# Attention and experts on one core: weights of the next units converted early and parked in DRAM, one stream of work units, sink fill moved ahead of the branch

## The chip, the cores and the metric

One core of one Trainium2 chip runs the whole program. The metric is the device time of one execution in microseconds (us). Its engines work side by side and meet through semaphores: TensorE (PE, matmuls), VectorE (DVE), ScalarE (ACT), GpSimd (POOL) and SyncE (SP), whose queue issues all DMAs here. Each engine works through its own queue in a fixed order.

## The reference

Three layers follow each other, all in float32 at the interface:

```python
# attention: 2 batches, 8 heads, 768 positions, head size 64; 4 sinks, window 128
scores = scale * np.matmul(q, k.transpose(0, 1, 3, 2))
keep = is_sink | in_window
a = softmax(np.where(keep, scores, -1e9))
x = (a @ v), reshaped to 1536 tokens x 512

# first layer: w_in 512 x 2048, w_out 2048 x 512, both given in float64
h = x @ w_in
g = h * np.tanh(softplus(h))          # mish
x = g @ w_out

# second layer: 4 experts, w1 512 x 1024, w2 1024 x 512, weighted by p
out += p[:, e:e+1] * (np.maximum(x @ w1[e], 0) @ w2[e])
```

## The kernel before

**Words.** Every matmul of the two last layers is done as three matmuls of parts: a number is split into a high part, which TensorE's fast float32 format holds, and a low part (`hi`, `lo`; names ending in h and l). So each weight matrix lies in SBUF twice. The first layer's weights come as float64. `split_double` (line 99) turns 1 MB of them into two parts of 512 KB by bit operations: one Abs on ACT (line 112), seven steps on DVE (lines 113 to 115 and 117 to 120), and a transfer of the high part (line 116) from the buffer `cv_h` to its place. This is called a conversion here. The buffers `cv_a`, `cv_r` and `cv_h` exist once.

**Attention.** It runs over 24 items: 2 batches, 3 blocks of 256 rows (i = 0, 1, 2), 4 pairs of heads. An item (`attention_item`, line 209) has four score matmuls (`sc`), a masked minimum on DVE (line 228), Exp on ACT, a reciprocal on DVE, the multiplication by it on POOL (lines 246 and 249), transposes (`tp`), and the products with v and with the sinks' v (`pv`). It ends with `xl` on DVE (line 179), by which items can be told in the trace. Its loads of q, k and v are asked for two items ahead. The sinks' v is filled and loaded by `sink_values` (line 132), within the branch that the flag in line 653 selects.

**Work units.** The first layer is cut into units 0 to 3 of 512 hidden columns, the second into units 4 to 11. One unit needs a first matrix `wi` (`wih`, `wil`) and a second, `wo`. `stream` (line 434) interleaves layer 1 of one chunk of tokens with layer 2 of the chunk before: chunks of 256, 256, 512 and 512 tokens for unit 0, three of 512 for all others. Layer 1 (line 450) makes four blocks `h` of 128 hidden columns, 12 matmuls each, in PSUM; `mish` (line 528) turns each into `gh` and `gl`: five activations on ACT with three DVE steps between them (540, 542, 543; the last one, `w`, is the last reader of `h`), then gh on ACT and gl on POOL. Layer 2 makes blocks `o` of 12 matmuls from the four gh and gl. Unit 0 runs within the attention from item 5 on, with one PSUM bank for h and one for o; after it there are three each. A pool of four pairs of g tiles serves the attention; three more are added behind it (`more_g`).

**Weights before.** While the attention runs, unit 0's four conversions and the two of unit 1's wi are asked for (m < 4, 8, 11). The two of unit 1's wo, and all eight of units 2 and 3, come behind it, the latter while the unit before runs (`rest`, line 591). The conversions write straight into SBUF; units 0 and 2 share one set of places, 1 and 3 the other.

**Order.** A scheduler with a model of the engines' times sets the order of each queue when the program is built. The source above gives it the dependencies and the priorities.

## Time and profile before

| | us |
|---|---|
| median of 3 runs (lowest, highest) | 960.02 (959.64, 961.45) |
| profiled execution | 957.99 |
| its span | 956.1 |
| PE busy | 922.4 (96%) |
| DVE busy | 421.3 (44%) |
| ACT busy | 350.1 (37%) |
| POOL busy | 273.4 (29%) |

The span is cut into 40 slices of 23.9 us on the profile's page. From 350 us to the last slice TensorE's digit is 9 in all of them; the lower ones all lie before. The attention's last DVE step starts at 173 us, the first matmul of the second layer's products (L515) at 445 us. In a stretch, PEclk is the granted TensorE clock as a share of full speed: 1.00 is 2.4 GHz, 0.50 is 1.2 GHz, and a value between is a mixture of both. A busy PE counts from an instruction's start to its modelled end, so a busy share near 100% can hide slower work.

### The profile page before, as it was taken

Reading aid. Unit: us, or ns where it says so; the run is one execution under the profiler, and the core shown is the slowest. Engines: PE = TensorE matmul, PEld = TensorE weight load, DVE = VectorE, ACT = ScalarE, POOL = GpSimd, SP = SyncE. Lnnn points to the kernel's source line nnn. Section 1 sums busy time; section 2 is a strip of 40 time slices with the busy share of each in tenths; the row PEclk is TensorE's granted clock in tenths of the full one; section 3 lists DMA queues with packets and bytes.
Section 4 is the critical chain, followed back from the end, with each engine's and each line's share of the span. In section 5 each row is a group of like instructions: output and inputs, shape, how many; then the busy total and the mean of one; then the engine's idle time right before and its main releaser. Section 6 shows DMA issues by size and latency. Waiting matters only on the chain.

```text
span 956.1 us, 11114 instructions
## 1 busy us (share of the span) xinstructions
PE 922.4 (96%) x4292; PEld 737.6 (77%) x4292; DVE 421.3 (44%) x754; ACT 350.1 (37%) x745; POOL 273.4 (29%) x233
## 2 busy tenths in 40 slices
PE   8998999878899999999999999999999999999997
PEld 5566577657688788888888888888888888888886
DVE  6898732189859745673112222222222222222222
ACT  4686774477576667852221111111111111111110
POOL 5786831122132245343022211220220222200000
PEclk7798999989899999999999999999999999999999
DMA  7654500033403101011011011110110110000012
GB/s 233 228 190 159 195 18 1 1 113 129 155 23 133 66 23 45 23 45 45 0 45 45 8 38 45 44 41 4 45 45 1 44 45 1 1 1 1 11 45 81
DMA packets 31198, 57.59 MB, mean 60 GB/s; under 512 B 3856, under 2 KB 12304, under 8 KB 31136
## 3 DMA queue, kind: packets, MB, share of 16 engines
q1 hardware_dynamic: 31136, 56.79, 17.9%
q8 instruction: 36, 0.59, 0.3%
q14 instruction: 26, 0.21, 0.1%
HBM read 45.25 MB, written 3.15 MB: 51 GB/s over the span
## 4 chain that ended last, share of the span: by engine, by line
PE 83%; DVE 11%; issue 2%; DMA 1%; ACT 1%; POOL 1%; SPq 0%; DVEq 0%; POOLq 0%; ACTq 0%
PE h L462 38%; PE o L515 27%; PE o L491 9%; PE sc L225 3%; PE pv L271 3%; PE tp L258 2%; DVE cv_h L115 2%; DVE cv_a L119 1%; DVE u L542 1%; DVE cv_a L117 1%; DVE w L543 1%; PE pv L277 1%; DVE u L540 1%; DVE cv_r L118 1%; DVE wol L120 1%
## 5 line engine op out<-in xcount | busy, mean ns | idle before, releaser
L462 PE MATMUL h<-xh,wih 128*128 128x512 f32 (+1 forms) x592 | 231.0, 390 | 13.0 <-DVE w L543 12.6
L462 PE MATMUL h<-xh,wil 128*128 128x512 f32 (+1 forms) x592 | 228.9, 387 | 0.0
L462 PE MATMUL h<-xl,wih 128*128 128x512 f32 (+1 forms) x592 | 228.1, 387 | 0.0
L473 ACT ACTIVATE gh<-h 128x512 fp32r<-128x512 f32 x96 | 57.3, 598 | 408.3 <-PE h L462 243.5
L474 DVE SCALAR_TENSOR_TENSOR gl<-h,gh 128x512 fp32r<-128x512 f32 x96 | 66.3, 692 | 207.8 <-ACT gh L473 207.8
L515 PE MATMUL o<-wol,gh 128*128 128x512 f32 (+1 forms) x388 | 150.1, 387 | 0.0
L515 PE MATMUL o<-woh,gh 128*128 128x512 f32 (+1 forms) x388 | 150.1, 387 | 0.0
L515 PE MATMUL o<-woh,gl 128*128 128x512 f32 (+1 forms) x388 | 149.9, 387 | 0.0
L462 PEld LDWEIGHTS h<-xh,wih 128*128 128x128 f32 x592 | 112.6, 190 | 39.7 <-DVE w L543 15.4
L523 DVE SCALAR_TENSOR_TENSOR acc<-o,pn,acc 128x512 f32<-128x512 f32 (+1 forms) x85 | 63.3, 745 | 176.2 <-PE o L515 176.2
L462 PEld LDWEIGHTS h<-xl,wih 128*128 128x128 f32 x592 | 112.3, 190 | 23.3 <-issue 1.1
L462 PEld LDWEIGHTS h<-xh,wil 128*128 128x128 f32 x592 | 112.6, 190 | 21.7
L96 POOL TENSOR_TENSOR gl<-w,gh 128x512 fp32r<-128x512 f32 (+1 forms) x52 | 69.7, 1344 | 186.8 <-ACT gh L88 182.9
L491 PE MATMUL o<-gh,woh 128*128 128x512 f32 (+1 forms) x208 | 79.6, 383 | 5.5 <-ACT gh L88 5.4
L515 PEld LDWEIGHTS o<-wol,gh 128*128 128x128 f32 x388 | 72.9, 188 | 14.9
L515 PEld LDWEIGHTS o<-woh,gh 128*128 128x128 f32 x388 | 72.9, 188 | 14.9
L515 PEld LDWEIGHTS o<-woh,gl 128*128 128x128 f32 x388 | 72.8, 188 | 14.7
L491 PE MATMUL o<-gh,wol 128*128 128x512 f32 (+1 forms) x208 | 78.5, 378 | 0.0
L491 PE MATMUL o<-gl,woh 128*128 128x512 f32 (+1 forms) x208 | 73.9, 380 | 0.0
L86 POOL TENSOR_SCALAR wih<-stage 128x1024 fp32r<-128x1024 f32 x16 | 16.5, 1052 | 193.7 <-PE h L462 193.7
L540 DVE SCALAR_TENSOR_TENSOR u<-w,r 128x512 f32<-128x512 f32 (+1 forms) x52 | 33.4, 643 | 64.4 <-ACT r L539 64.3
L86 POOL TENSOR_SCALAR woh<-stage 128x1024 fp32r<-128x1024 f32 x16 | 16.5, 1053 | 137.1 <-PE o L515 122.1
(82 smaller groups left out, 1125.3 us busy)
## 6 DMA issues: line engine op xcount, KB each, us to landing
stage<-in_moe_w_dram SPq DMA_DIRECT2D x32, 512.0 KB, 3.7
stage<-in_moe_w_in_dram SPq DMA_DIRECT2D x8, 1024.0 KB, 5.8
stage<-in_moe_w_out_dram SPq DMA_DIRECT2D x8, 1024.0 KB, 5.0
qk<-in_qk_dram SPq DMA_DIRECT2D x16, 324.0 KB, 3.3
wih<-cv_h SPq DMA_DIRECT2D x8, 512.0 KB, 3.2
woh<-cv_h SPq DMA_DIRECT2D x8, 512.0 KB, 2.9
acc<-in_v_dram SPq DMA_DIRECT2D x16, 192.0 KB, 2.6
out_dram<-acc SPq DMA_DIRECT2D x11, 256.0 KB, 2.1
```

The source lines that it names most:

```text
L86: eng.tensor_scalar(out, src, 1.0, 0.0, ALU.mult, ALU.add)
L96: eng_lo.tensor_tensor(lo, src, hi.bitcast(F32), ALU.subtract)
L115: nc.vector.scalar_tensor_tensor(h, w_hi, -0x40000000, a, ALU.bitwise_and, ALU.bitwise_or)
L225: nc.tensor.matmul(sc, lhsT=raw[rows, t * P:(t + 1) * P], rhs=raw[rows, k0:k0 + sw], start=True, stop=True)
L271: nc.tensor.matmul(pv[64 * j:64 * j + 64, q0:q0 + ns * P], lhsT=v[:, blk, j * c.D:(j + 1) * c.D], rhs=pts[j][:, sg:sg + ns], start=n == 0, ...
L462: nc.tensor.matmul(h, lhsT=wis[sw][:, k, fs], rhs=x[sx][:, k, cols], start=k == 0 and t == 0, stop=k == KT - 1 and t == 2,)
L473: nc.scalar.activation(gh, h, AF.Relu)
L474: nc.vector.scalar_tensor_tensor(gl, h, 0.0, gh.bitcast(F32), ALU.max, ALU.subtract)
L491: nc.tensor.matmul(o, lhsT=wos[sw][:, f, ds], rhs=g[f][sx], start=f == 0 and t == 0, stop=f == NF - 1 and t == 2,)
L515: nc.tensor.matmul(o, lhsT=g[f][sx][:, ds], rhs=wos[sw][:, f, ms], start=f == 0 and t == 0, stop=f == NF - 1 and t == 2,)
L523: nc.vector.scalar_tensor_tensor(y, o, pcol, y, ALU.mult, ALU.add)
L540: nc.vector.scalar_tensor_tensor(u, w, 1.0, r, ALU.add, ALU.mult)
```

## The change

- **Parking.** A new `park` converts unit 1's wi and wo and unit 2's wi, six conversions, while the attention runs (items 8, 10, 12, 14, 16 and 18), and writes both halves to DRAM. `split_double` gets a buffer `cv_l` for the low half and one more transfer (line 126 of the kernel after). `weights` loads the halves back (line 434), two transfers of 512 KB per conversion. Unit 2's wo and unit 3's weights are converted as before.
- **Space.** Unit 1's wi no longer lies in SBUF during the attention; both its matrices are placed behind it. All seven pairs of g tiles exist from the start.
- **One stream.** Unit 0's chunks and all later units form one stream.
- **Sinks.** `sink_values` is called ahead of the branch.
- **Softmax multiplies.** For items with i = 0 the two multiplies of the first head of the pair go to DVE, those of the second stay on POOL.

```diff
@@ split_double
+    park = lo
+    if lo.dtype != F32R:
+        lo = pool.tile([P, n], F32R, tag="cv_l", name="cv_l")
...
-    nc.sync.dma_start(out=hi.bitcast(F32), in_=h.bitcast(F32))
+    nc.sync.dma_start(out=hi if lo is not park else hi.bitcast(F32), in_=h.bitcast(F32))
...
     nc.vector.scalar_tensor_tensor(lo, af, 2.0 ** -23, rf, ALU.mult, ALU.mult)
+    if lo is not park:
+        nc.sync.dma_start(out=park, in_=lo.bitcast(F32))
@@ attention_pools
-    a.vsk = sink_values(c, a)
+    a.vsk = c.vsk
@@ attention_item
-                nc.gpsimd.tensor_scalar(o, o, sm[:, 2 * j + t:2 * j + t + 1], None, ALU.mult)
+                (nc.gpsimd if j else nc.vector).tensor_scalar(o, o, sm[:, 2 * j + t:2 * j + t + 1], None, ALU.mult)
@@ Experts
-        self.gp = []
-        self.more_g(ctx, 4)
+        self.gp = ctx.enter_context(tp(name="m_g", bufs=7))
...
+    def park(self, pool, n, nm):
+
+        w = self.units[n][2 + (nm == "wo")]
+        hi, lo = self.parked[n, nm] = [pool.tile([P, self.KT, self.FU], F32, name=f"{nm}{n}{x}") for x in "hl"]
+        for k in range(0, self.KT, 2):
+            split_double(self.c, self.cv, hi[:, k:k + 2], lo[:, k:k + 2], load_double(self.c, w, k))
+            yield
...
+            if (n, nm) in self.parked:
+                for k in range(0, KT, 2):
+                    for t, d in zip((hi, lo), self.parked[n, nm]):
+                        nc.sync.dma_start(out=t[:, k:k + 2].bitcast(F32), in_=d[:, k:k + 2])
+                    yield
+            elif kind == 0:
@@ banded
-    x.wpool[1]["wi"] = ctx.enter_context(tc.tile_pool(name="m_1wi", bufs=1))
-    w = chain(x.weights(0), x.weights(1))
+    w = x.weights(0)
...
-    steps = x.stream([(0, 0, QW), (0, QW, QW)] + [(0, t0, x.CW) for t0 in range(2 * QW, c.T, x.CW)])
+    steps = x.stream([(0, 0, QW), (0, QW, QW)] + [(0, t0, x.CW) for t0 in range(2 * QW, c.T, x.CW)] + later(c, x, 1))
+    dram = ctx.enter_context(tc.tile_pool(name="park", bufs=1, space=bass.MemoryType.DRAM))
+    w = chain(w, x.park(dram, 1, "wi"), x.park(dram, 1, "wo"), x.park(dram, 2, "wi"))
...
-        if m < 4 or m in (8, 11):
+        if m < 4 or m in PARK:
...
-    x.wpool[1]["wo"] = ctx.enter_context(tc.tile_pool(name="m_1wo", bufs=1))
-    x.more_g(ctx, 3)
+    x.wpool[1] = ctx.enter_context(tc.tile_pool(name="m_w1", bufs=1))
     x.psum(ctx, 3, 3, 2)
-    run(w)
-    run(steps)
-    rest(c, x)
+    run(x.weights(1))
+    run(steps, 4 * (x.NF + 4) - 4 - (len(items) - LAG))
+    rest(c, x, steps, 1)
@@ swa_mish_experts_kernel, ahead of the branch
     mask_parts(c)
+    c.vsk = sink_values(c)
```

What this does to the order is seen best on DVE. First, the scores of item 18 in DVE's queue, before (L228 is the masked minimum of one score tile, `pr`; L542 and L543 are mish of a block of unit 0; the small second row of each minimum is left out):

```order
L228 ISA pr_1519,mx_1520<-sc_1522,mask260_90 128x260
L228 ISA pr_1519,mx_1520<-sc_1526,mask260_90 128x260
L542 SCALAR_TENSOR_TENSOR u_827<-u_827,r_828 128x256
L543 SCALAR_TENSOR_TENSOR w_826<-u_827,h_811 128x256
L228 ISA pr_1519,mx_1520<-sc_1530,mask260_90 128x260
L228 ISA pr_1519,mx_1520<-sc_1534,mask260_90 128x260
L179 TENSOR_TENSOR xl_92<-pv_1266,xh_91 128x256
```

And the scores of item 18 now (L234 is the same minimum, L117 to L123 are steps of a conversion):

```order
L117 TENSOR_SCALAR cv_a_1292<-cv_a_1292 128x1024
L234 ISA pr_1568,mx_1569<-sc_1571,mask260_90 128x260
L118 TENSOR_SCALAR cv_a_1292<-cv_a_1292 128x1024
L234 ISA pr_1568,mx_1569<-sc_1575,mask260_90 128x260
L119 SCALAR_TENSOR_TENSOR cv_h_1294<-stage_60,cv_a_1292 128x1024
L240 RECIPROCAL sm_1486<-sm_1486 128x4
L121 TENSOR_SCALAR cv_a_1292<-cv_h_1294 128x1024
L122 TENSOR_SCALAR cv_r_1293<-cv_h_1294 128x1024
L123 SCALAR_TENSOR_TENSOR cv_a_1292<-stage_60,cv_a_1292 128x1024
```

Between the scores of one item there stand five or more steps of a conversion now, where none stood.

Second, DVE's queue behind the attention, from mish of the first block of unit 0's last chunk on, before (wol is unit 1's second matrix, low half):

```order
L120 SCALAR_TENSOR_TENSOR wol_1997<-cv_a_1999,cv_r_2000 128x1024
L540 SCALAR_TENSOR_TENSOR u_2054<-w_2053,r_2055 128x512
L113 TENSOR_SCALAR cv_a_2012<-cv_a_2012 128x1024
L542 SCALAR_TENSOR_TENSOR u_2054<-u_2054,r_2055 128x512
L114 TENSOR_SCALAR cv_a_2012<-cv_a_2012 128x1024
L543 SCALAR_TENSOR_TENSOR w_2053<-u_2054,h_2038 128x512
L115 SCALAR_TENSOR_TENSOR cv_h_2014<-stage_60,cv_a_2012 128x1024
L117 TENSOR_SCALAR cv_a_2012<-cv_h_2014 128x1024
L118 TENSOR_SCALAR cv_r_2013<-cv_h_2014 128x1024
L540 SCALAR_TENSOR_TENSOR u_2082<-w_2081,r_2083 128x512
L119 SCALAR_TENSOR_TENSOR cv_a_2012<-stage_60,cv_a_2012 128x1024
```

The same place now (L553, L555 and L556 are the three steps of mish):

```order
L553 SCALAR_TENSOR_TENSOR u_2099<-w_2098,r_2100 128x512
L555 SCALAR_TENSOR_TENSOR u_2099<-u_2099,r_2100 128x512
L556 SCALAR_TENSOR_TENSOR w_2098<-u_2099,h_2083 128x512
L553 SCALAR_TENSOR_TENSOR u_2127<-w_2126,r_2128 128x512
L555 SCALAR_TENSOR_TENSOR u_2127<-u_2127,r_2128 128x512
L556 SCALAR_TENSOR_TENSOR w_2126<-u_2127,h_2111 128x512
```

The conversion steps between the steps of mish are gone from this place; the next one (L124) stands behind mish of the third block of unit 1.

Third, SP's queue at the end of the attention, before (the last loads of q, k and v, then the high halves of unit 1's wo):

```order
L128 DMA qk_1754<-in_qk_dram 128x648
L202 DMA acc_59<-in_v_dram 128x3x128 x3
L116 DMA woh_1996<-cv_h_2001 128x1024
L116 DMA woh_1996<-cv_h_2014 128x1024
L366 DMA stage_60<-in_moe_w_in_dram 128x2x1024
```

And now (wi2l and the like are the parked halves in DRAM):

```order
L120 DMA wi2h_1450<-cv_h_1625 128x1024
L372 DMA stage_60<-in_moe_w_out_dram 128x2x1024
L126 DMA wi2l_1451<-cv_l_1622 128x1024
L372 DMA stage_60<-in_moe_w_in_dram 128x2x1024
L434 DMA wih_2057<-wi1h_792 128x1024
L434 DMA wil_2058<-wi1l_793 128x1024
```

Eight loads of unit 1 follow each other from there, behind one load of unit 3's words into the staging buffer, and then the four of unit 2's wi.

## Rows read from the trace of the kernel before

**Rows 1.** Stretches: us, busy us of PE, PEld, DVE, ACT, POOL, clock, DMA.

```profile
33.12:69.69 36.57, 35.76 (x225) 22.87 (x224) 33.22 (x92) 30.07 (x95) 26.75 (x29) 0.99 0.66 224
77.42:147.39 69.97, 67.25 (x455) 48.59 (x455) 42.52 (x146) 53.94 (x171) 44.39 (x57) 0.95 0.35 113
173.00:260.00 87.00, 70.45 (x284) 55.76 (x285) 63.82 (x78) 55.50 (x93) 19.82 (x13) 0.92 0.29 100
260.00:350.00 90.00, 88.44 (x388) 72.24 (x388) 64.95 (x91) 60.09 (x100) 22.92 (x17) 1.00 0.18 67
```

**Rows 2.** TensorE in order of time: start, us, instruction, [idle before, and its releaser].

```profile
185.33 0.50 PE L462 MATMUL h<-xh,wih 128*128 128x512 f32 x1 [1.64 <-DVE w L543]
...
195.76 0.79 PE L491 MATMUL o<-gh,woh 128*128 128x512 f32 x1 [5.36 <-ACT gh L88]
...
199.96 0.80 PE L462 MATMUL h<-xh,wih 128*128 128x512 f32 x1
...
207.62 0.40 PE L462 MATMUL h<-xh,wih 128*128 128x512 f32 x1
...
216.75 0.50 PE L462 MATMUL h<-xh,wih 128*128 128x512 f32 x1 [3.51 <-DVE w L543]
...
227.96 0.50 PE L462 MATMUL h<-xh,wih 128*128 128x512 f32 x1 [1.40 <-DVE w L543]
...
249.81 0.79 PE L462 MATMUL h<-xh,wih 128*128 128x512 f32 x1 [4.55 <-DVE w L543]
...
320.35 0.50 PE L462 MATMUL h<-xh,wih 128*128 128x512 f32 x1 [1.46 <-DVE w L543]
```

**Rows 3.** Chain of waits, 196 to 270 us: start, us, what it was.

```profile
212.63 1.13 DVE cv_a L119
...
235.99 6.56 DMA woh<-cv_h
...
249.81 5.49 PE h L462 x12
...
255.30 1.72 PE o L491 x6
...
264.92 2.72 PE h L462 x12
```

**Rows 4.** Conversions: six steps' DVE time; L118's group; L117's durations in ns.

```profile
0.00:350.00 350.00, 107.62 (x96) 0.94 0.33 112
...
L118 DVE TENSOR_SCALAR cv_r<-cv_h 128x1024 int32<-128x1024 int32 x16 | 12.3, 766 | 0.0
...
L117 DVE TENSOR_SCALAR cv_a<-cv_h x16: 677/736/1674, 20.9 to 314.9; 128x1024 int32<-128x1024 int32 x16
```

**Rows 5.** ACT in time at the attention's end, and the chain of waits there.

```profile
177.74 1.15 ACT L88 ACTIVATE gh<-w 128x512 fp32r<-128x512 f32 x2 [4.70 <-PE o L491]
...
179.78 0.61 ACT w L536
...
184.58 0.70 DVE w L543
```

**Rows 6.** DMA issues: KB each, median us from issue to landing.

```profile
stage<-in_moe_w_in_dram SPq DMA_DIRECT2D x8, 1024.0 KB, 5.8
```

**Rows 7.** DVE in order of time, last step of items 20 and 23.

```profile
147.39 0.42 DVE L179 TENSOR_TENSOR xl<-pv,xh 128x256 fp32r<-128x256 f32 x1 [0.32 <-ACT xh L178]
...
173.08 0.42 DVE L179 TENSOR_TENSOR xl<-pv,xh 128x256 fp32r<-128x256 f32 x1 [0.95 <-ACT xh L178]
```

**Rows 8.** Waits of TensorE for POOL's multiplies: us, times, longest.

```profile
PE tp L258 <- POOL pr L246: 1.7, 3, 0.8
```

**Rows 9.** SP's queue and the chain of waits at the start.

```profile
9.24 0.75 SPq L140 DMA_DIRECT2D acc<-in_vsink_dram  x2
...
10.61 6.24 DMA qk<-in_qk_dram
```

More of the change, by code (lines that the diff above doesn't have):

```diff
@@ L30 @@
 WARM = 12
+PARK = (8, 10, 12, 14, 16, 18)
 class Ctx:
@@ L129, in load_item, with sink_values @@
     return raw
-def sink_values(c, a):
+def sink_values(c):
     nc = c.nc
@@ L383, in __init__ @@
         self.acc = c.acc
-        self.wpool = [{nm: ctx.enter_context(tp(name=f"m_0{nm}", bufs=1)) for nm in ("wi", "wo")}, {}]
+        self.wpool = [ctx.enter_context(tp(name="m_w0", bufs=1)), None]
         self.cv = ctx.enter_context(tp(name="m_cv", bufs=1))
         self.tp = ctx.enter_context(tp(name="m_t", bufs=2))
-        self.gp = []
-        self.more_g(ctx, 4)
+        self.gp = ctx.enter_context(tp(name="m_g", bufs=7))
         self.units = []
@@ L398, in __init__ @@
         self.w = {}
-    def more_g(self, ctx, n):
-        self.gp += n * [ctx.enter_context(self.c.tc.tile_pool(name=f"m_g{n}", bufs=n))]
+        self.parked = {}
     def psum(self, ctx, nh, no, nr=0):
@@ L414, in weights @@
         FU, KT = self.FU, self.KT
+        wp = self.wpool[n % 2]
         res = self.w[n] = []
         for nm, w in (("wi", wi), ("wo", wo)):
-            wp = self.wpool[n % 2][nm]
             hi = wp.tile([P, KT, FU], F32R, tag=f"{nm}h", name=f"{nm}h")
@@ L420, in weights @@
             res.append((hi, lo))
-            if kind == 0:
+            if (n, nm) in self.parked:
[4 more added lines that the diff above has]
+            elif kind == 0:
                 for k in range(0, KT, 2):
@@ L465, in layer1 @@
                     )
-            gp = self.gp.pop(0)
-            self.gp.append(gp)
-            gh = gp.tile([P, self.CW], F32R, tag="gh", name="gh")[:, 0:cw]
-            gl = gp.tile([P, self.CW], F32R, tag="gl", name="gl")[:, 0:cw]
+            gh = self.gp.tile([P, self.CW], F32R, tag="gh", name="gh")[:, 0:cw]
+            gl = self.gp.tile([P, self.CW], F32R, tag="gl", name="gl")[:, 0:cw]
             if kind == 0:
@@ L582, in banded, with later, rest @@
     first.close()
-    x.wpool[1]["wo"] = ctx.enter_context(tc.tile_pool(name="m_1wo", bufs=1))
-    x.more_g(ctx, 3)
+    x.wpool[1] = ctx.enter_context(tc.tile_pool(name="m_w1", bufs=1))
     x.psum(ctx, 3, 3, 2)
-    run(w)
-    run(steps)
-    rest(c, x)
-def rest(c, x, first=1):
+    run(x.weights(1))
+    run(steps, 4 * (x.NF + 4) - 4 - (len(items) - LAG))
+    rest(c, x, steps, 1)
+def later(c, x, first):
+    return [(n, t0, x.CW) for n in range(first, len(x.units)) for t0 in range(0, c.T, x.CW)]
+def rest(c, x, steps, first):
     per = (c.T // x.CW) * (x.NF + 4)
-    units = range(first, len(x.units))
-    steps = x.stream([(n, t0, x.CW) for n in units for t0 in range(0, c.T, x.CW)])
-    for n in units:
+    for n in range(first, len(x.units)):
         w = x.weights(n + 1) if n + 1 < len(x.units) else iter(())
@@ L609, in dense @@
     x = Experts(c, ctx)
-    x.wpool[1] = {nm: ctx.enter_context(c.tc.tile_pool(name=f"m_1{nm}", bufs=1)) for nm in ("wi", "wo")}
-    x.more_g(ctx, 3)
     w = x.weights(0)
+    x.wpool[1] = ctx.enter_context(c.tc.tile_pool(name="m_w1", bufs=1))
     x.psum(ctx, 3, 3, 2)
     run(w)
-    rest(c, x, 0)
+    rest(c, x, x.stream(later(c, x, 0)), 0)
 @with_exitstack
```

## The prediction, made before the changed kernel ran

> **What bounds the kernel now.** I read the stretches first. From 350 us on TensorE is busy in every slice, with all weights in time, so nothing is to be won there. Before that, three stages differ [rows 1]. While items 2 to 7 of the attention run (33.12 to 69.69), DVE is busy 33.22 of 36.57 us, 91%. While items 8 to 20 run (77.42 to 147.39), it is busy 42.52 of 69.97 us, 61%, and TensorE 67.25. From 173 to 260 TensorE is busy only 70.45 of 87 us and the mean clock is 0.92; from 260 to 350, 88.44 of 90.
>
> Second, the instructions before which TensorE stood idle after the attention [rows 2]: 1.64 + 5.36 + 3.51 + 1.40 + 4.55 + 1.46 = 17.9 us. Five of the six (12.6 us) wait for the last product of mish on DVE (w, L543), since a PSUM bank of h comes free only then; the 5.36 waits for gh.
>
> Third, the chain of waits says why w is late [rows 3]: between 196 and 250 us conversion steps of unit 1's wo and unit 2's weights stand in DVE's queue between the steps of mish (L119 at 212.63), and a transfer of converted words takes 6.56 us from 235.99. The long waits are followed by matmuls at half clock (1.2 instead of 2.4 GHz): 12 matmuls take 5.49 us from 249.81, against 2.72 from 264.92, and 6 take 1.72 from 255.30, where half of 2.72 is 1.36: 3.1 us. After the 5.36 wait nine matmuls run from 195.76 to 199.96 [rows 2], 4.20 us, where nine of 12 by 2.72 are 2.04.
>
> **The change, part by part.**
>
> *Conversions that leave the stage behind the attention.* One conversion has seven DVE steps; 16 conversions take 107.62 + 12.3 us, 7.5 us each [rows 4]. By the order of the instructions, DVE has 64 such steps behind item 20 before and 45 now, and between there and the end of unit 0 only mish stands in its queue. The waits of 3.51, 1.40 and 4.55 us and the 3.1 us of half clock lie where the removed steps stood: -12.6 us. The 1.46 before 320.35 comes behind four conversions in a row, for unit 3; these now have unit 1's time too, from 210 us on: -1.46. Six conversions stay (unit 2's wo, unit 3). The last step of the first of them waits for TensorE to be through with unit 0's wo, with mish of unit 1's fourth block queued behind it on DVE; some 48 matmuls, 11 us, stand in TensorE's queue before that block is read, against some 7 us (5.5 up to w [rows 5], and gh and gl behind it). Nearest row for such a clump: 1.46. I take +2, and 0 to 7.7 (4.55 + 3.1, if one clump is still as bad) as ends.
>
> *Seven g tiles from the start.* Before, four pairs exist until the attention ends; gh of the second-last chunk's blocks waits 4.70 us for layer 2 of the chunk before to release them [rows 5], POOL's gl and the w tile follow, and TensorE's 1.64 at 185.33 ends this chain. With seven it doesn't wait: between the third and the fourth block stand 12 matmuls of 256 and 21 of 512 columns, 6.1 us at 2.72 for 12 of 512, against 5.5 us of mish up to w (179.78 to 185.28). -1.64. The 5.36 stays: mish of the fourth block has the same steps, shared with the next block's, and the same nine matmuls cover it. So do its slow matmuls.
>
> *One stream for all units.* The order moves nothing at the seam: before, too, unit 1's first block stands among unit 0's last layer 2. Nothing.
>
> Behind the attention: -12.6 - 1.46 - 1.64 + 2 = -13.7 us.
>
> *Reloading.* Unit 1's halves come back in eight transfers of 512 KB, unit 2's wi in four. The first eight stand on SP behind one load whose buffer DVE frees before the attention ends, and wait for the attention's space, free at about 173. 1 MB lands in 5.8 us [rows 6], so by that row all 4 MB are there some 23 us later, at 196, and wi, the first half, at 185; its first matmul stands in TensorE's queue where unit 1 began before, at 207.62 [rows 2]. Cover 11 to 20 us, cost nothing; were it gone, up to 10 us. Nothing else of the next 20 us stands behind them on SP.
>
> *Conversions that enter the attention.* Between the x of item 8 and that of item 20 DVE has 38 conversion steps now and 14 before: 24 more, 3.4 conversions, 25.7 us at 7.5 each. At the shortest durations (0.68 for L117, where 0.74 is the median) it is about 6.3 each, 21.6. Eight multiplies of softmax come too, of 384 columns per pair: by 0.68 for 1,024 columns, 0.25 us a pair at least and 1.35 at most; 0.5 each, 2 us. So DVE needs 66 to 70 us where it needed 42.5, and the stage has 70. It would be paced by DVE as items 2 to 7 are: at their 91%, 73 to 77 us, +3 to +7. I take +5, since POOL, which lengthens these steps, is less busy here (44.39 of 70 us, against 26.75 of 36.57) [rows 1]. Ends: 0, if all goes into DVE's idle time; +17.8, if an item takes 7.31 us as items 2 to 7 do (36.57 / 5; 12 items 87.8). The rest, items 21 to 23, is TensorE's: 25.7 us from 147.39 to 173.08 [rows 7], with the work of 62 matmuls of unit 0 (512 columns) in it before and 61.5 now. ACT gets 3.4 more Abs of about 1.1 us, with 16 us idle in the stage; SP six more writes of lo, each waiting for the conversion's last step, with loads for q, k and v behind it that are asked for two items ahead (2 x 5.83 us) against 7.5 us of conversion. Nothing for both.
>
> A rule of the Trainium skill speaks against this part. In the row, L117 takes 677 ns at least and 1674 at most [rows 4], the long ones beside POOL work. The Trainium skill (SBUF — State Buffer, Who interferes with whom) says that DVE and GpSimd share a port pair under an exclusive lock, so that the second to start blocks fully. By the row's longest case for each of the 24 steps that would be 24 us more, not 5; in the sum it has no part.
>
> *Multiplies off POOL.* Half of the softmax multiplies of the i = 0 items go to DVE. TensorE waited 1.7 us for them [rows 8]; -1.7, and 0 as the other end.
>
> *Sink fill ahead of the branch.* SP issues the two sink transfers at 9.24 for 0.75 us, ahead of the qk load with which the chain begins at 10.61 [rows 9]. Now they go out before the branch, while SP waits for the flag: -0.75.
>
> **Sum.** -13.7 + 5 - 1.7 - 0.75 = -11.1. The profiled execution took 957.99 us (span 956.1, 1.9 around it): 946.9. The median of the three runs is 2.03 above it, so 948.9; I say 949.0.
>
> **The rivals.** *The attention takes it all for nothing.* DVE idles 27 us of items 8 to 20. For it: TensorE is busy there 96%, and has matmuls of unit 0 to put anywhere. Against it: scores need DVE between two matmuls, and DVE would have to be full. 949.0 - 5 = 944.
>
> *DVE sets the pace (slower).* Items 8 to 20 go at 7.31 us, +17.8, and POOL's relief is worth nothing because its work blocks the same: 957.99 + 2.03 - 13.7 - 0.75 + 17.8 = 963.4. For it: the 91% of rows 1 and the long L117; the rule of the skill above would work this way. It decides from 12 items in 84.4 us, 7.04 each (14.45 us more). Against it: items 2 to 7 also have DVE steps lengthened by more POOL work.
>
> *The waits behind the attention stay.* Six conversions are enough to hold mish up once as before 249.81: 4.55 + 3.1 kept, 949.0 + 7.7 = 956.7. For it: conversion steps and mish share one queue and the first conversion waits for TensorE. Against it: four conversions from 285 to 320 cost 1.46.
>
> *Unit 1's weights are late.* TensorE waits up to 10 us for wi: 959. Against it: the cover above.
>
> **How the numbers follow.** Forecast (945 to 955) 0.5; attention for nothing, 944, 0.18; DVE sets the pace, 963.4, 0.14; waits stay, 956.7, 0.12; weights late, 959, 0.06. A measurement of this kernel can tell some 0.2% (1.9 us) from no change, so faster means under 958.1 and slower over 961.9. Faster: 0.5 + 0.18 + 0.10 of the fourth = 0.78. Slower: most of the pace case, 0.13, and a bit of late weights: 0.14. Same: the rest, 0.08. The range of 943 to 960 leaves out the pace case and the ends of the first two, less than 0.2.
>
> **What would show it.** Right: no wait of TensorE for w between 200 and 270 us, and no half clock there but after the one wait of about 5.4; x of item 20 some 2 to 3 us later than 147.4 (5 - 1.7 - 0.75); last pv at 174 to 178; wi of unit 1 landed 10 us before its first matmul; TensorE's end about 11 us earlier. Wrong: x of item 20 later than 157, waits of TensorE for scores or for softmax summing to over 10 us from 77 on, a clock below 1.0 from 110 to 170, or a wait of TensorE for wih.

## The result: 3% faster, more than twice the forecast gain

| | before | after |
|---|---|---|
| median in us (lowest to highest, executions) | 959.83 (957.47 to 961.45, 4) | 931.44 (930.07 to 933.54, 4) |
| profiled execution, span | 957.99, 956.1 | 931.33, 929.5 |

The ratio is 0.9708 with an interval of 0.9681 to 0.9735. The forecast was 949.0 with a range of 943 to 960: the sign is right, the gain is 28.4 us where 10.8 were forecast, and the time lies 11.6 us below the range. The profiled executions differ by 26.66, their spans by 26.6; that is what has to be found.

Both traces can be cut at the same two events: the end of the attention's last `xl`, and the end of `gh` of the fourth 512-column block of unit 0's second chunk (at 195.71 before, for which the 5.36 us wait of [rows 2] stands, and at 184.73 after). TensorE has nearly the same number of matmul records in each piece. The stretches view of the kernel before, with the columns of [rows 1] (the number of records in brackets):

```profile
0.00:173.50 173.50, 162.67 (x961) 111.85 (x962) 111.72 (x335) 115.28 (x353) 101.00 (x125) 0.91 0.43 141
173.50:195.71 22.21, 15.27 (x72) 12.18 (x70) 4.81 (x8) 10.24 (x19) 3.84 (x3) 0.97 0.01 4
195.71:956.10 760.39, 744.43 (x3261) 613.59 (x3261) 304.73 (x413) 224.55 (x374) 168.55 (x105) 0.99 0.13 43
```

The same three pieces of the kernel after, and below them its items 2 to 7 and 8 to 20, which answer the first two lines of [rows 1], and 251 to 341 us:

```profile
0.00:164.28 164.28, 150.68 (x960) 105.78 (x961) 142.75 (x379) 118.79 (x359) 95.41 (x110) 0.96 0.61 206
164.28:184.73 20.45, 15.15 (x73) 12.29 (x71) 4.14 (x7) 9.03 (x18) 2.57 (x2) 0.99 0.01 2
184.73:929.50 744.77, 739.81 (x3261) 612.57 (x3261) 277.70 (x385) 219.93 (x370) 165.71 (x105) 0.99 0.13 44
...
30.37:68.61 38.24, 34.94 (x221) 22.95 (x222) 38.20 (x101) 31.45 (x99) 30.24 (x31) 0.96 0.65 216
75.70:143.22 67.52, 65.56 (x449) 46.75 (x450) 66.20 (x176) 55.49 (x173) 43.85 (x48) 0.97 0.70 240
251.00:341.00 90.00, 90.00 (x399) 74.53 (x398) 66.99 (x91) 63.40 (x107) 31.07 (x22) 1.00 0.20 71
```

| piece | measured | forecast for it |
|---|---|---|
| A, the attention | 164.28 - 173.50 = -9.2 | +5 - 1.7 - 0.75 = +2.55 |
| B, up to the fourth gh | 20.45 - 22.21 = -1.8 | -1.64 |
| C, the rest | 744.77 - 760.39 = -15.6 | -12.6 - 1.46 + 2 = -12.06 |

In C TensorE's idle time fell from 15.96 us (760.39 - 744.43) to 4.96, and its busy time by 4.6 for the same 3,261 matmuls. In A idle time did not fall, it rose from 10.83 to 13.60; TensorE's busy time fell by 12.0 for the same matmuls, with the granted clock at 0.96 instead of 0.91. So the conversions' departure did what it should in C, and three quarters of the surprise in these two executions (11.8 of 15.5 us) lie in A, for which the forecast had a small loss.

TensorE after, in order of time, with the wait that answers the 5.36 of [rows 2] and unit 1's first matmul (207.62 before):

```profile
184.78 0.79 PE L504 MATMUL o<-gh,woh 128*128 128x512 f32 x1 [5.35 <-ACT gh L89]
...
196.68 0.39 PE L477 MATMUL h<-xh,wih 128*128 128x512 f32 x1
```

The waits view of TensorE for all that follows 164.28 (us, times, longest) has only this line:

```profile
PE o L504 <- ACT gh L89: 5.4, 1, 5.4
```

The five waits for w in [rows 2] are gone. The chain of waits, which in [rows 3] went through conversion steps, runs from 184.78 on through TensorE's own work alone:

```profile
183.38 0.70 DVE w L556
184.10 0.64 ACT gh L89
184.78 4.21 PE o L504 x9
188.99 3.76 PE h L477 x12
...
196.84 2.72 PE h L477 x12
```

### The profile page after: what moved, and what is told of

The parts are those of the page before. It is cut to its first block, busy times and chain, and to the rows that moved or that the text cites. A ratio compares the mean times of both kernels' runs of the same rounds, so it can differ in the third digit from the quotient of the medians.

```text
span 929.5 us, 11138 instructions
## 1 busy us (share of the span) xinstructions
PE 905.6 (97%) x4292; PEld 730.6 (79%) x4292; DVE 424.6 (46%) x770; ACT 347.7 (37%) x745; POOL 263.7 (28%) x217
## 4 chain that ended last, share of the span: by engine, by line
PE 86%; DVE 10%; ACT 1%; DMA 1%; issue 0%; POOL 0%; DVEq 0%; ACTq 0%
PE h L477 42%; PE o L528 28%; PE o L504 14%; DVE pr L234 2%; DVE cv_h L119 1%; DVE cv_a L123 1%; PE pv L277 1%; DVE cv_a L117 1%; DVE cv_r L122 1%; DMA stage<-in_moe_w_in_dram 1%; PE sc L231 1%; PE tp L264 1%; DVE cv_a L121 1%; DVE xl L185 1%; DVE cv_a L118 0%
## 5 line engine op out<-in xcount | busy, mean ns | idle before, releaser
L504 PE MATMUL o<-gl,woh 128*128 128x512 f32 (+1 forms) x208 | 77.4, 379 | 0.0
L553 DVE SCALAR_TENSOR_TENSOR u<-w,r 128x512 f32<-128x512 f32 (+1 forms) x52 | 34.4, 662 | 50.2 <-ACT r L552 49.9
```

Of the source, the lines that this page charges most:

```text
L504: nc.tensor.matmul(o, lhsT=wos[sw][:, f, ds], rhs=g[f][sx], start=f == 0 and t == 0, stop=f == NF - 1 and t == 2,)
L553: nc.vector.scalar_tensor_tensor(u, w, 1.0, r, ALU.add, ALU.mult)
```

## The experiments

Theories at the start: (P) the parking explains the gain, and acts behind the attention; (S) the other, small edits explain what the forecast lacks; later (O), the order in which the planner puts unit 0's work among the attention's items, and TensorE's clock that goes with it, explains A. Every ratio is to the kernel before on the same chip. The table has the three pieces of each profiled execution, in us, with TensorE's granted clock in A. Where the number of matmul records in A differs from 960, some of unit 0's work has moved between A and B, so there A and B are read together. Each row is a single execution and can lie some us from the median: e8's, at 959.68, is the slowest of its ten.

| kernel | median | A, clock | B | C | A + B |
|---|---|---|---|---|---|
| before | 959.8 | 173.50, 0.91 | 22.21 | 760.39 | 195.7 |
| after | 931.4 | 164.28, 0.96 | 20.45 | 744.77 | 184.7 |
| e13, after again | 934.2 | 166.41, 0.93 | 20.47 | 743.22 | 186.9 |
| e1, start parts alone | 953.2 | 169.12, 0.92 | 19.48 | 760.60 | 188.6 |
| e2, parking alone | 949.8 | 174.18, 0.90 | 30.09 | 743.43 | 204.3 |
| e3, sink in the branch | 964.4 | 187.73, 0.84 | 25.81 | 750.46 | 213.5 |
| e4, multiplies on POOL | 952.5 | 177.11, 0.88 | 30.58 | 744.91 | 207.7 |
| e5, before, longer warm-up, order kept | 961.4 | 172.90, 0.94 | 22.21 | 760.79 | 195.1 |
| e6, after, one more warm-up matmul | 953.4 | 171.66, 0.91 | 35.88 | 744.26 | 207.5 |
| e7, after, the other head's multiplies | 956.0 | 172.91, 0.89 | 30.28 | 751.01 | 203.2 |
| e8, before, one more warm-up matmul | 954.9 | 177.91, 0.88 | 19.49 | 760.50 | 197.4 |
| e9, e7 with two waits filled | 951.6 | 168.24, 0.91 | 30.27 | 751.09 | 198.5 |
| e10, after, the 5.35 wait filled | 934.0 | 170.39, 0.91 | 20.49 | 743.22 | 190.9 |
| e11, after, parked steps narrow | 929.8 | 165.68, 0.91 | 20.49 | 743.23 | 186.2 |
| e12, after, four g tiles | 948.9 | 175.03, 0.90 | 22.37 | 750.50 | 197.4 |
| e16, after, two blocks later | 936.1 | 169.30, 0.94 | 19.09 | 744.31 | 188.4 |
| e17, after, five g tiles | 938.2 | 166.70, 0.93 | 20.64 | 748.96 | 187.3 |
| e18, after, two streams | 938.3 | 170.81, 0.91 | 20.46 | 747.43 | 191.3 |

### The parts of the change, alone and undone

**e1**: the kernel before with the sink fill ahead of the branch and the multiplies shared.

```diff
+    c.vsk = sink_values(c)
-    a.vsk = sink_values(c, a)
+    a.vsk = c.vsk
-                nc.gpsimd.tensor_scalar(o, o, sm[:, 2 * j + t:2 * j + t + 1], None, ALU.mult)
+                (nc.gpsimd if j else nc.vector).tensor_scalar(o, o, sm[:, 2 * j + t:2 * j + t + 1], None, ALU.mult)
```

> The kernel before with the two edits that act on the start alone: sink fill ahead of the branch, and half of the i = 0 multiplies on DVE. No conversion is parked, the streams stay apart, four g tiles stay. Theory S (the start was under-sized: TensorE gets full clock some 10 us earlier, and items 0 to 3 are not held up by POOL): x of item 8 some 2 us earlier and the attention's end 5 to 9 us earlier than 173.1, so 951 to 955 against 959.8. Rival P (the prediction's terms, -0.75 and -1.7): 957.4. Behind the attention both expect the waits of 3.5, 1.4 and 4.6 us unchanged.

**e2**: the changed kernel without these two edits, so the parking, the tiles and the one stream.

> The changed kernel with its two edits on the start undone: sink fill back inside the branch, all multiplies on POOL. Parking, the one stream and seven g tiles stay. Theory S: what the start parts give (5 to 8 us) is lost, so 936 to 940. Rival P: 2.45 lost, 933.9. A third reading, that the two edits only help because DVE and POOL are loaded anew by the parking, expects the same loss here as S but nothing in the kernel before with them alone.

**e3** and **e4**: the changed kernel with only the sink fill, or only the multiplies, put back.

> The changed kernel with the sink fill alone put back inside the branch. Theory S (clock): TensorE pauses again between its warm-up and the first scores, is at half clock from about 12 to 32 us, and the end is 4 to 6 us later, 935 to 937. Rival P: only the two transfers' issue time, 0.75, so 932.2.

> The changed kernel with all multiplies of the i = 0 items on POOL again. If POOL's relief is what moved items 0 to 3 and 12 to 15 ahead: 3 to 5 us later, 934 to 936. Rival P: 1.7 later, 933.1. If DVE is the bound of the attention, these eight pairs of multiplies cost DVE what they save POOL, and it is within 1 us of 931.4 or earlier.

Measured: e1 953.2 (ratio 0.9929, 0.9900 to 0.9957), e2 949.8 (0.9890, 0.9869 to 0.9911), e3 964.4 (1.0036, 1.0008 to 1.0064), e4 952.5 (0.9915, 0.9875 to 0.9955). The two small edits are worth 6.6 us on the kernel before (forecast 2.45), but undoing the sink fill alone costs 33 us, the multiplies alone 21, both together only 18. e1 came where S had it, but e2, e3 and e4 lie far above what either theory had (932 to 940). Such numbers don't add up to parts of a sum, so S falls as it stood. C sorts them: 760.4 to 760.6 without parking, 743 to 751 with it, and all the rest of the differences is in A and B. P holds for C and for nothing else. e3's A shows how an order loses: TensorE runs at 0.66 from 50 to 75 us, and the low clock begins behind two waits for the minimum of the scores. The stretch of e3, and two of its matmuls in time; the second stands ahead of another stretch at half clock, from 82 to 92 us:

```profile
50.00:75.00 25.00, 23.12 (x101) 14.68 (x103) 16.47 (x44) 15.56 (x48) 12.56 (x16) 0.66 0.48 161
```

```profile
58.11 1.23 PE L231 MATMUL sc<-qk 64*128 64x260 f32 x2 [1.12 <-DVE mx L234]
...
81.49 0.48 PE L231 MATMUL sc<-qk 64*128 64x128 f32 x2 [1.62 <-DVE mx L234]
```

### Edits that should do nothing

**e6** and **e8**: one more matmul of 0.4 us in the warm-up ahead of the attention, in after and in before. **e7**: the multiplies that went to DVE are the second head's instead of the first's. In each the planner makes a new order; e6 moves some 1,650 lines of TensorE's list, e8 some 530.

```diff
-WARM = 12
+WARM = 13
```

```diff
-                (nc.gpsimd if j else nc.vector).tensor_scalar(o, o, sm[:, 2 * j + t:2 * j + t + 1], None, ALU.mult)
+                (nc.vector if j else nc.gpsimd).tensor_scalar(o, o, sm[:, 2 * j + t:2 * j + t + 1], None, ALU.mult)
```

> The changed kernel with one more warm-up matmul, 0.4 us of work, planned anew: some 1,650 of TensorE's rows stand elsewhere. Order theory (the 28 us are in part the fortune of one order): not 931.4 but, as in the kernels with single edits undone, 945 to 955, with 12 to 25 us of TensorE's work at half clock (in equivalents of full clock) against 10. Rival (the edits have their own worth in any order): 931 to 933.

> The kernel before with one more warm-up matmul, planned anew: some 530 of TensorE's rows stand elsewhere. Order theory: off 959.8 by 4 us or more to either side. Rival: 959 to 961.

> The changed kernel with the other half of the i = 0 multiplies on DVE (head 1 in place of head 0): the same work on each engine, planned anew. Order theory: anywhere from 928 to 955, set by how long TensorE is at half clock. Rival: 931 to 933.

Measured: e6 953.4 (0.9885, 0.9829 to 0.9942), e8 954.9 (0.9948, 0.9932 to 0.9963), e7 956.0 (0.9945, 0.9909 to 0.9981). An edit of 0.4 us takes 22 us from the changed kernel and gives the kernel before 5. The stretches of e6:

```profile
0.00:171.66 171.66, 155.04 (x927) 105.41 (x928) 141.73 (x374) 114.44 (x350) 92.28 (x109) 0.91 0.59 197
171.66:207.54 35.88, 24.46 (x109) 19.64 (x107) 7.60 (x12) 13.96 (x27) 3.85 (x3) 0.88 0.01 3
207.54:951.80 744.26, 739.30 (x3261) 612.29 (x3261) 278.35 (x385) 220.25 (x370) 166.03 (x105) 1.00 0.13 44
```

C is that of after. A holds 927 matmuls instead of 960: fewer of unit 0's were put into the attention, and B holds 109 instead of 73; there mish and TensorE wait in turn (11.4 us idle of 35.88). **e13**, the changed kernel run again on another chip, shows that its own order is steadily good: 934.2 (931.9 to 936.0), ratio 0.9737 (0.9709 to 0.9765).

> The changed kernel itself once more, on another chip. If the time belongs to its order: 930 to 934, as in the two kernels that kept its order (934.0 and 929.8). If it was the chip and the moment: 940 to 955.

### The order held fixed

In these the order of all queues stays, and only single instructions are repeated or made smaller in it. **e5** adds four warm-up matmuls to the kernel before, **e9** fills two waits of e7 (12 and 14 repeated matmuls), **e10** fills the 5.35 us wait of after with 22.

In the diffs, in this order, the helpers copy matmuls within TensorE's finished list (the row to copy, the row behind which the copies go, their number).

```diff
+    lengthen_warm(nc, 4)
```

```diff
+    repeat_matmul(nc, 190, 201, 12)
+    repeat_matmul(nc, 46, 53, 14)
```

```diff
+    repeat_matmul(nc, 750, 750, 22)
```

> The kernel before with four more warm-up matmuls, put in after its order was fixed, so that every other instruction stands where it stood: they fill 1.8 us in which TensorE waited before 9.73. Clock theory: the fall to half clock moves from about 10 to about 16 us, as it stands in each kernel with the sink fill ahead, the attention ends 2 to 5 us earlier than 173.1, 955 to 958. Rival (order alone: where the fill stands matters only since it lets the planner order all that follows anew): the clock does not move the end, 959 to 960.

> The kernel with mirrored multiplies, its order as it was, with 14 and 12 matmuls more that repeat a product into a sum still open (so the output is off): they fill two waits of TensorE, of 1.80 us at 31.59 for POOL and of 1.44 at 77.30 for DVE, behind which the clock stood at half from 31 to 52 and from 79 to 87 us. Clock theory (a wait of 1 to 2 us brings TensorE to half clock, and at half clock it is the bound of the attention): no half clock from 31 to 52, the attention ends some 8 to 13 us earlier than 172.5, 943 to 948. Rival (in the attention other engines set the pace and the clock is only a symptom, as in the run with four more warm-up matmuls): 955 to 957 whatever the clock.

> The changed kernel, its order as it was, with 22 matmuls more that repeat a product into a sum still open (so the output is off), in TensorE's 5.35 us wait for gh at 184.78. Clock theory: no half clock from 184 to 191, 3.4 us of TensorE's work back, 927.5 to 929. Rival: the wait is what costs, not the clock: 931 to 932.

**e5**: 961.4 (1.0005, 0.9987 to 1.0022). The first fall came at 12.5 us instead of 10.4, not at 16 as expected. The clock came back early, 1.00 in 28 to 32 us against 0.50 before, but TensorE's idle time in A rose from 10.83 to 13.95 and A became only 0.6 shorter: DVE is busy 3.93 and POOL 3.88 of these 4 us, so DVE and POOL, not TensorE, seem to set the pace there. Stretches of before and then of e5:

```profile
28.00:32.00 4.00, 4.00 (x14) 2.15 (x13) 3.76 (x8) 1.82 (x7) 4.00 (x4) 0.50 0.14 56
```

```profile
28.00:32.00 4.00, 3.35 (x21) 1.86 (x19) 3.93 (x9) 3.12 (x12) 3.88 (x2) 1.00 0.54 182
```

**e9**: 951.6 (0.9918, 0.9891 to 0.9945), against 956.0 for e7. In e7 TensorE waits 1.80 us and then runs at half clock for 21 us; with the wait filled the same stretch runs at 1.00 with 131 records instead of 75. First e7, the wait and then the stretch:

```profile
31.59 0.69 PE L264 MATMUL tp<-ident,pr 128*128 128x128 f32 x2 [1.80 <-POOL pr L252]
```

```profile
31.00:52.00 21.00, 19.97 (x75) 11.60 (x76) 14.79 (x43) 11.35 (x35) 9.11 (x12) 0.51 0.54 181
```

Then e9, the stretch and its next wait:

```profile
31.00:52.00 21.00, 19.22 (x131) 12.61 (x131) 20.00 (x58) 16.68 (x51) 14.46 (x16) 1.00 0.78 252
```

```profile
54.83 1.58 PE L231 MATMUL sc<-qk 64*128 64x260 f32 x4 [1.63 <-DVE mx L234]
```

The items were 5.7 us earlier, but the clock fell again, from 54 to 68, next to the new wait of 1.63 at 54.83; 4.4 us of it reached the end (A is 4.7 shorter). The time lies between the two readings of the expectation. The intervals of the two ratios overlap, but of e9's six runs only one, at 954.7, reaches e7's seven (954.1 to 957.5). So in this order the clock in the attention costs time, some microseconds for 21 us at half clock; that is the part of O that a run bears out.

**e10**: 934.0 (0.9727, 0.9691 to 0.9762), as e13. The half clock behind the wait of 5.35 went away, and B and C stayed as in e13, 20.49 and 743.22: TensorE now waited 0.37 and 1.04 us for mish instead. So against e13 the half clock behind this wait, some 3 us there, costs nothing; after, which has 7 us of it, has a C 1.55 longer, less than the 3.4 expected. The stretch behind the wait in after and in e10, and then e10's two waits:

```profile
184.00:192.00 8.00, 7.22 (x19) 5.68 (x20) 2.86 (x6) 7.08 (x14) 2.57 (x2) 0.57 0.90 302
```

```profile
190.00:198.00 8.00, 6.58 (x28) 4.74 (x27) 2.96 (x5) 6.93 (x14) 2.59 (x2) 1.00 0.86 294
```

```profile
190.93 0.50 PE L504 MATMUL o<-gh,woh 128*128 128x512 f32 x1 [0.37 <-ACT gh L89]
...
194.32 0.50 PE L477 MATMUL h<-xh,wih 128*128 128x512 f32 x1 [1.04 <-DVE w L556]
```

**e11** prices the conversions in the attention. Four DVE steps of each of the six parked conversions (lines 117, 118, 121 and 123) work on 64 of 1,024 columns.

```diff
+    narrow_parked(nc, 64, "lrh")
```

> The changed kernel, its order as it was, with four of the seven DVE steps of each of the six parked conversions cut from 1024 to 64 columns (so the parked words are off): 2.9 us of DVE less for each, 17 us in all between 70 and 140 us. The prediction's term (+5 for 25.7 us of steps): 3 to 4 us earlier, 927 to 928.5. Rival 1 (the attention takes the conversions for nothing, since TensorE sets its pace): 930.5 to 932. Rival 2 (DVE, busy 97% there, sets the pace): 915 to 922.

Measured: 929.8 (0.9682, 0.9646 to 0.9718). DVE is busy 125.36 us in A instead of 143 to 144. Its A against that of e10, which has the same order and as much half clock in A (some 31 us in each, summed over stretches of 1 us), is 4.7 us shorter:

```profile
0.00:165.68 165.68, 155.47 (x960) 109.96 (x961) 125.36 (x379) 118.83 (x359) 88.04 (x110) 0.91 0.61 205
```

```profile
0.00:170.39 170.39, 158.62 (x960) 111.24 (x961) 144.06 (x379) 118.87 (x359) 94.70 (x110) 0.91 0.60 199
```

So 18.7 us of DVE work removed shorten the attention by 4.7, in one execution against another; in proportion, 25.7 us would be worth 6.5 (an estimate). The forecast's +5 was of the right size. The intervals of the whole times overlap, though none of e11's four runs (928.1 to 931.2) reaches e10's (932.5 to 935.9).

### Tiles, streams and the waiting block

**e12** gives four g tiles in the attention and three behind it, as before; **e17** five of them in all; **e18** separates unit 0's stream from the later units' as before; **e16** takes two blocks of unit 0 out of the attention's last two items. The diffs stand in this order.

```diff
-        self.gp = ctx.enter_context(tp(name="m_g", bufs=7))
+        self.gp = []
+        self.more_g(ctx, 4)
...
+    x.more_g(ctx, 3)
```

```diff
-        self.gp = ctx.enter_context(tp(name="m_g", bufs=7))
+        self.gp = ctx.enter_context(tp(name="m_g", bufs=5))
```

```diff
-    steps = x.stream([(0, 0, QW), (0, QW, QW)] + [(0, t0, x.CW) for t0 in range(2 * QW, c.T, x.CW)] + later(c, x, 1))
+    steps = x.stream([(0, 0, QW), (0, QW, QW)] + [(0, t0, x.CW) for t0 in range(2 * QW, c.T, x.CW)])
-    rest(c, x, steps, 1)
+    run(steps)
+    rest(c, x, x.stream(later(c, x, 1)), 1)
```

```diff
-        if m >= LAG:
+        if LAG <= m < len(items) - 2:
...
```

> The changed kernel with four pairs of g tiles while the attention runs and three more behind it, as before; planned anew. The prediction's term: a wait of 1 to 2 us for w comes back before the fourth block of the last but one chunk of unit 0, 933. Order theory: 945 to 960, by the time at half clock.

> The changed kernel with five pairs of g tiles in place of seven; TensorE's order is the same up to the end of the attention. If the number of tiles is what counts: gh of a 512-column block waits some us for a tile, and the end is 3 to 9 us later, 937 to 943. Rival (the run with four tiles lost by the order of items 14 to 23): 932 to 935.

> The changed kernel with unit 0's steps run to their end before those of the other units are set up, as before; TensorE's order is the same up to about 190 us. The prediction's term: nothing, 932 to 935. Rival: the last layer 2 of unit 0 finds no block of unit 1 between its steps, a wait of 3 to 6 us at the seam, 935 to 941.

> The changed kernel with the last two blocks of unit 0's second chunk taken behind the attention's loop, so that they get PSUM banks of the later pool in place of one shared bank; the order up to item 17 stays. If that chain makes the wait of 5.35 us: it goes, with the half clock behind it (3.4 us), 923 to 928. Rival (mish of the last block sets it whatever the bank): the wait stays, 930 to 934.

**e12**: 948.9 (0.9874, 0.9832 to 0.9915). Its order is that of after up to about item 14, so here a difference can be traced. ACT's gh in e12 wait for layer 2, as [rows 5] showed for before; in after the first two of the four are done during the attention:

```profile
179.41 1.15 ACT L89 ACTIVATE gh<-w 128x512 fp32r<-128x512 f32 x2 [4.83 <-PE o L511]
186.98 0.63 ACT L89 ACTIVATE gh<-w 128x512 fp32r<-128x512 f32 x1 [1.55 <-DVE w L563]
196.77 0.63 ACT L89 ACTIVATE gh<-w 128x512 fp32r<-128x512 f32 x1 [1.55 <-DVE w L563]
```

```profile
151.13 0.62 ACT L89 ACTIVATE gh<-w 128x512 fp32r<-128x512 f32 x1
163.72 0.62 ACT L89 ACTIVATE gh<-w 128x512 fp32r<-128x512 f32 x1
174.37 0.63 ACT L89 ACTIVATE gh<-w 128x512 fp32r<-128x512 f32 x1 [1.55 <-DVE w L556]
184.10 0.63 ACT L89 ACTIVATE gh<-w 128x512 fp32r<-128x512 f32 x1 [1.55 <-DVE w L556]
```

e12's B is 1.9 us longer than after's (22.37 to 20.45), the size forecast for the tiles, and TensorE's wait for w is back in it, 1.65 us at 187.01; C is 7.3 longer than e13's, and A 4.6 longer than e10's at nearly the same clock. Together that is some 14 us for the tiles, not 1.64, with the order that came with them: from item 14 on e12's differs, and how much of the 14 is the order's was not separated. **e17**: 938.2 (0.9771, 0.9744 to 0.9798), A and B as in e13, C 5.7 longer. **e18**: 938.3 (0.9775, 0.9735 to 0.9815), C 4.2 longer; its order is after's up to about 190 us. The intervals of both overlap with e13's; what is clear is C, which four executions of after's order have at 743.2 to 744.8. Both have the same three waits behind the attention that after has not; from e17's TensorE in time, and the chain of waits there:

```profile
231.70 0.50 PE L477 MATMUL h<-xh,wih 128*128 128x512 f32 x1 [0.33 <-DVE w L556]
...
240.60 0.50 PE L504 MATMUL o<-gh,woh 128*128 128x512 f32 x1 [1.13 <-DVE acc L512]
...
300.43 0.50 PE L477 MATMUL h<-xh,wih 128*128 128x512 f32 x1 [1.45 <-DVE w L556]
```

```profile
234.69 2.21 DVE cv_h L119
...
238.22 1.13 DVE cv_a L123
```

These are 2.9 us of waits next to conversions: the first next to the second one of unit 2's wo, the other two next to those of unit 3's weights. The forecast had +2 for the clump of unit 2's wo and took unit 3's for free (its -1.46). Such waits are real in other orders too (3.1 us of C in e3, 4.9 in e7, 4.3 in e12), and after's own order escapes them. **e16**: 936.1 (0.9750, 0.9715 to 0.9785): the 5.35 wait is 3.99 there, B 1.4 shorter, and the total no better; A is 169.30. In this run the wait is shorter and the time stays.

### Without the planner's model

**e14** and **e15** are before and after with the order of the source instead of the planner's.

```diff
-    with _tile.TileContext(nc, schedule_with_timeline_sim=True) as tc:
+    with _tile.TileContext(nc, schedule_with_timeline_sim=False) as tc:
```

> The kernel before, ordered by the planner without its simulated times (one more warm-up matmul then changes no other row). Slower or faster than 959.8 by an unknown amount, 950 to 1010; it is the base for the next run.

> The changed kernel, ordered by the planner without its simulated times. Order theory (the change's own worth is about the forecast's 11 us, the rest is the fortune of one order): 6 to 15 us less than the kernel before with that planner. Rival (the change is worth 28 us in any order): 24 to 32 us less.

Measured: 995.8 (1.0375, 1.0354 to 1.0396) and 982.2 (1.0223, 1.0198 to 1.0247). The change gives 13.6 us here, near the 10.8 that were forecast. TensorE's clock in A is 0.78 in e14 and 0.80 in e15. A and B sum to 236.9 in e14 and 228.1 in e15, C takes 757.0 and 755.0; but 50 matmuls more stand in e15's C, some 11 us at 2.72 for 12. For equal work e15's C is thus some 13 us shorter and its A and B some 2.5 longer (an estimate; the two profiled spans differ by 10.8): here too the gain lies behind the attention.

## Why the prediction was right in sign and wrong in size

**Behind the attention (C): right, 3.6 us too small.** The waits of 3.51, 1.40 and 4.55 and the 1.46 went, and the half clock behind the 4.55 with them; C is 760.4 to 760.8 in the four kernels of the table that don't park and 743 to 751 in all that do. Idle time fell by 11.0, as the 10.92 of these waits; busy time fell by 4.6, where the half clock had been priced at 3.1; and the residual +2 did not come in this order: these two make the 3.6. In other orders such waits came, 2.9 in e17 and e18. Undoing the one stream, priced at nothing, costs 4.2 us of C (e18), so the step "the order moves nothing at the seam" failed for this order. But e3, e7, e12 and e17 have the one stream and such waits as well: which mish stands beside the later conversions is a matter of the whole order.

**Fourth block (B): right**, -1.8 against -1.64, and the wait of 5.36 stayed as 5.35 with its slow matmuls, as said. That those slow matmuls cost little or nothing (e10) wasn't foreseen.

**Weights back from DRAM: right in cost, wrong in the wait.** TensorE waits for no weight; unit 1 began at 196.68 instead of 207.62. But the loads did not go out when the attention's space came free at its end, 164.3: SP stood before the first of them for 35.2 us, until a step of mish was through at 183.3. By their times to landing (4.8 to 6.5 us) all of wi was there at some 191, 6 us before its first use, where the forecast had 11 to 20. SP's wait (us, times, longest) and the first load:

```profile
SPq L434 <- DVE u L555: 35.2, 1, 35.2
```

```profile
183.42 0.34 SPq L434 DMA_DIRECT2D wih<-wi1h  x1
```

**Conversions in the attention: right in size, wrong in its reason.** The forecast took 91% busy for DVE's ceiling. After, DVE is busy 38.20 of 38.24 us in items 2 to 7 and 66.20 of 67.52 in items 8 to 20. The 66 to 70 us of DVE work that were forecast there were 66.2, and the price was some 5 us (e11); the rest went into DVE's idle time. Nor did the conversions' steps get longer in sum: the same six steps of all 16 took 107.74 us, where [rows 4] had 107.62, although POOL was busy 43.85 of the 67.52 us to which they were added. The stretch of these steps in the kernel after:

```profile
0.00:350.00 350.00, 107.74 (x96) 0.97 0.41 142
```

The Trainium skill (SBUF — State Buffer, Who interferes with whom) says that DVE and GpSimd share a port pair under an exclusive lock, and that, of two instructions that need it, the one that issues first fully blocks the other. The 24 us that the forecast gave for the worst case of that rule did not come. That single steps are blocked is not excluded: the longest of L118 in the kernel after took 1.72 us, at a median of 0.69 (1.71 and 0.72 for this step before).

**The attention as a whole (A): this step failed.** The forecast added up DVE's and POOL's waits and the sink fill's issue, +2.55, and left TensorE's side of the attention as it was: "The rest, items 21 to 23, is TensorE's", with the same work, and no term for the clock in A. The time fell by 9.2 instead, in two parts. (TensorE's idle time rose by 2.8, close to the 2.55, but only by 0.9 in e10, so that is luck.) The last steps of items 20 and 23 after, which answer [rows 7], and the same two of e10, whose clock in A is 0.91 as before's, with some 31 us at half clock in both:

```profile
143.22 0.41 DVE L185 TENSOR_TENSOR xl<-pv,xh 128x256 fp32r<-128x256 f32 x1
...
163.86 0.42 DVE L185 TENSOR_TENSOR xl<-pv,xh 128x256 fp32r<-128x256 f32 x1 [0.33 <-ACT xh L184]
```

```profile
149.57 0.41 DVE L185 TENSOR_TENSOR xl<-pv,xh 128x256 fp32r<-128x256 f32 x1
...
169.97 0.42 DVE L185 TENSOR_TENSOR xl<-pv,xh 128x256 fp32r<-128x256 f32 x1 [0.34 <-ACT xh L184]
```

At before's clock item 20 ends at 149.57, 2.2 later than the 147.39 of before, which is what the forecast said (2 to 3). From there to item 23 it takes 20.40 us in e10 and 20.64 in after, against 25.69: TensorE has 135 records there in after where it had 147, all at 1.00 in both kernels; 42 of them, not 51, are of unit 0's h in 512 columns. The forecast had the same work there, since the same number of these matmuls stands between the items' `pv` in both lists. But when DVE ends item 20, TensorE is now further on in its list: 11 of the h matmuls in 512 columns have run by then, 2 before. These nine are 2.2 of the 5.0 us (TensorE is busy 11.02 us with h there instead of 13.25). Another 2.3 come from work that is the same, 48 `pv` matmuls in 5.60 instead of 7.38 us and 27 of o in 3.94 instead of 4.50; in the new list `pv` stands in longer runs, which may be why (no run isolates it). This makes A 3.1 us shorter at the same clock, 5.7 below the forecast. The other 6.1 are the clock of the one execution that was profiled: it has some 14 us of half clock in A, e10 and before 31. The five executions of this order (after, e13, e17, e10, e18) have A from 164.28 to 170.81 with clocks of 0.96, 0.93, 0.93, 0.91 and 0.91, some 14, 24, 24, 31 and 31 us at half clock. So this part belongs to the execution and is luck; the same order run again had a median of 934.2 (e13), a gain of some 26 us. Most of the difference lies at the start: before is at half clock from 10 to 34 us, after from 17 to 24, e10 from 16 to 37. With the sink fill ahead of the branch the first fall came at 13 to 18 us in every kernel that the planner ordered, without it at 9 to 10 (e5, with its longer warm-up, at 12.5); the forecast priced this edit by its issue time alone. Before, and then after and e10:

```profile
10.00:34.00 24.00, 22.88 (x75) 12.36 (x74) 18.89 (x57) 14.93 (x50) 18.96 (x21) 0.50 0.80 280
```

```profile
16.00:37.00 21.00, 18.07 (x88) 10.17 (x89) 19.04 (x53) 15.06 (x45) 7.68 (x9) 0.84 0.81 287
```

```profile
16.00:37.00 21.00, 19.55 (x66) 10.80 (x66) 16.57 (x45) 11.45 (x33) 6.77 (x7) 0.51 0.72 254
```

In the middle of the attention, from 75 to 125 us, TensorE is fuller in the new order, at either clock; before, after and e10:

```profile
75.00:125.00 50.00, 45.77 (x302) 32.62 (x302) 35.52 (x111) 37.12 (x122) 34.30 (x40) 0.93 0.48 156
```

```profile
75.00:125.00 50.00, 49.05 (x345) 34.77 (x343) 48.75 (x134) 41.95 (x133) 30.06 (x33) 1.00 0.77 255
```

```profile
75.00:125.00 50.00, 48.27 (x320) 35.53 (x320) 47.03 (x126) 40.33 (x127) 28.82 (x32) 0.93 0.74 241
```

The planner had put more of unit 0's work there: in 512-column matmuls, 54 stand ahead of item 14's first `pv` in TensorE's list where 28 stood, 62 instead of 36 ahead of item 15's.

Of the signs that the forecast named, those on A went against it in this execution: x of item 20 came 4.2 us earlier than 147.4, not later, the last `pv` ended at 163.4 instead of 174 to 178, and the clock fell between 110 and 170 us (0.57 from 136 to 140). Only TensorE's waits for scores and softmax from 77 us on stayed small, some 1 us.

**What the change is worth apart from this order.** The six other orders with parking (e2, e3, e4, e6, e7, e12; e16, e17 and e18 keep most of after's) have a mean of 954.2, and A and B of 197 to 214 us against 195.7 before: by them, parking gives some 9 to 17 us in C and loses most of it in the attention again. The forecast, 949.0, lies at their lower end (948.9 to 964.4). What lifted the result to 931.4 is this one order, whose A and B, 184.7 to 191.3 in five executions, are the shortest of all seven. The forecast read in it where conversions and blocks of unit 0 stand, and did not count the 54 against 28 matmuls. A rival remains: e1, the two small edits without parking, has A and B of 188.6, as short as this order's. Added up as separate parts, its 6.6 us and the 15.6 of C make 22.2 of the 28.4. The runs e2, e3 and e4 speak against fixed parts, but they all have new orders; no run takes the small edits out of an order held fixed.

**The rivals.** "Attention for nothing" (944) comes nearest, but not for its reason: the conversions did cost what was said (e11). DVE did not set the pace of items 8 to 20 (4.7 us for 18.7 of its work), no wait for w stayed, no weight was late.

**Open.** Which of the waits in an order makes the clock fall, and why the half clock at the start lasts 7 us in one execution of an order and 20 in another, is not settled, nor why half clock costs time in one order (6.1 us for 17 in after's) and hardly any in another (0.6 for 10 in e5): e9 shows one such wait at work, e5 one that costs next to nothing. What the g tiles and the one stream are worth in other orders wasn't tried.

## What to carry to other kernels

When a scheduler makes the order, price a change in two sums: the work that it moves, and the order that comes with it. For the second, count in the new order how much filler stands ahead of each stage of the bounding engine, and let the range be as wide as edits that do nothing (here 0.4 us of warm-up, worth 22 us) make it. An undone edit tells what it is worth only if the order stays the same; so hold the order fixed and resize single instructions in it, and compare stages with equal numbers of records.

## What the hardware showed that was not expected

- Next to waits of TensorE of 1.1 to 1.8 us in the attention, the granted clock fell to 1.2 GHz for long stretches (21 us in e7, from 31 to 52; 17 in e3, from 58 to 75); with that wait of e7 filled, it stayed at 2.4 GHz until 54 us, next to a wait of 1.63.
- Half clock can be nearly free: e5 had some 10 us less of half clock at the start than before, and e10 3 us less than e13 behind the wait of 5.35, and neither changed the time. DVE and POOL were busy 98 and 97% in the one place, and TensorE waited for mish in the other.
- DVE was busy 98 to 100% for 38 and 68 us, and taking 18.7 us of its work away made the attention only 4.7 us shorter (e11): TensorE had matmuls of another layer to do meanwhile.
